# Queueing the late steps of an attention epilogue by estimated time

## The chip, the cores and the metric

The kernel runs on one NeuronCore of a Trainium2 chip, core 0. The metric is the device time of one launch in microseconds. A profiled execution gives the span and the records of every engine: TensorE (PE, with its weight loads as PEld), VectorE (DVE), ScalarE (ACT), GpSimd (POOL), and SyncE (SP), which issues the DMAs.

## The reference

Four transformer attention layers on a sequence of 2048 tokens with 512 features: 32 heads of 16 features. Layers 0 and 2 use the weights A and a sliding window of 256 keys; layers 1 and 3 use the weights B and attend to all 2048 keys, without a causal mask. Each layer adds its result to its input.

```python
def attn(x, wqkv, wo):                       # A: windowed, B: no mask
    qkv = (x @ wqkv).reshape(B, S, 3, H, Dh).transpose(2, 0, 3, 1, 4)
    q, k, v = qkv[0], qkv[1], qkv[2]
    scores = einsum("bhqd,bhkd->bhqk", q, k) * Dh ** -0.5
    mask = (idx[:, None] - idx[None, :] >= 0) & (idx[:, None] - idx[None, :] < 256)
    scores = where(mask[None, None], scores, -1e9)              # A only
    o = einsum("bhqk,bhkd->bhqd", softmax(scores), v)
    return o.transpose(0, 2, 1, 3).reshape(B, S, D) @ wo
x = A_x
for wqkv, wo in ((A_wqkv, A_wo), (B_wqkv, B_wo)) * 2:
    x = x + attn(layernorm(x), wqkv, wo)
```

## The kernel before

**Tiles.** The 2048 tokens are four chunks of 512 (`c` = 0 to 3), each of four token tiles of 128. The heads come in groups; one group of eight heads of one chunk, a quarter `t`, makes one `o` tile of 128 x 512. Names carry layer, chunk and part: `po2_3_1` is the output projection of layer 2, chunk 3, token tile 1. Numbers are split into a high and a low 16-bit half (`xh`, `oh`, `w`), so that a product takes three matmuls.

**One layer's work.** For a chunk: the layer norm (`st`, `mv`, the small operations of `rsqrt` in lines 44 to 51, then per tile `xn` and the two halves `xh`); `transpose` (PE `pt`, copies `xc`, high half by ACT, low half by DVE); `keys`, `queries`, `values` (PE `pq`, `pv`; halves `sp`, squares `sq`, norms of queries and keys `phq`, `phk`, from which DVE makes `km` and the shift `m`); attention (scores `s`, exponentials `e` by ACT, masks on POOL at L715 and L718 in the window layers, sums into one of two PSUM tiles `acc`); `epilogue`; and `wo` (PE `po`, then DVE `dx` = po x gcol at L567, and x + dx at L568). All of `pq`, `pv`, `po`, `pt` take a PSUM bank from the same small rotation, so a later one waits until DVE or ACT has read an earlier one.

**The epilogue.** It copies `acc` to `oe` (L599) and stores it; the denominators are read back as `lt`. Two later parts stand in a queue `late`. `reciprocals` makes the reciprocals on DVE and sends them through DRAM: `lt` to `rcp`, and `rcp` back, broadcast, as `r`. `normalised` multiplies `o` by `r` (L626) and splits the product into `oh` (L628, L629). In a window layer the first runs one step of the attention loop later, the second three; in a full layer three and five.

**The order.** PE's instruction order is written out by the program as it runs the loops; the other engines take their instructions in program order, moved by priorities in a few places. Beside the attention loop, `Side` holds a list of works for each chunk (`side0` for layer 0, and so on): transposes `T`, keys `K`, queries `Q`, values `VV`, output projections `OO`, norms `NN`, weight preparation `PR`. `Side.step` takes pieces of them between the steps of the attention, by their shares of cost. A work is taken when its dependencies are met by an estimated clock: `clock[0]`, which grows by an estimate for each piece; `ONR` holds the time from which `oh` counts as ready, and `XNR` the same for a norm. `Side.finish` takes what is left, and sets the clock forward when nothing is ready. The attention of a layer ends with `flush(0)` and `run_late(True)`, which forces all late parts; then `all_of` runs what must come before the next layer, the tail, for example values, the output projection of chunk 3, and the transposes and projections of the next layer's last chunk.

**Weights.** `maxima` finds column maxima (`wa` is a reduction over a weight's rows), `scales` makes powers of two, `parts` scales the weight (`wr`, on POOL), casts it to its high half (`w`, on DVE) and subtracts for the low half (POOL); one `yield` for each of four blocks. With `act` set the engines are DVE, ACT and POOL.

Of the kernel before, what the change touches and what calls it, by code (L numbers as in the profile page):

```python
# [38 lines left out]
def rsqrt(nc, vp, tag, var):  # L39

    v = vp.tile([P, 4], F32, name=f"v{tag}", tag="lnv")
    y = vp.tile([P, 4], F32, name=f"y{tag}", tag="lny")
    z = vp.tile([P, 4], F32, name=f"z{tag}", tag="lnz")
    nc.vector.tensor_scalar_add(v, var, EPS)
    nc.vector.tensor_scalar(y.bitcast(I32), v.bitcast(I32), 1, None, op0=ALU.logical_shift_right)
    nc.vector.tensor_scalar(y.bitcast(I32), y.bitcast(I32), -1, 0x5F3759DF, op0=ALU.mult, op1=ALU.add)
    for _ in range(3):
        nc.vector.tensor_mul(z, y, y)
# [141 lines left out]
def fast_path(ctx, tc, flag, a_x, a_wqkv, a_wo, b_wqkv, b_wo, out):  # L190
# [18 lines left out]
    CM, DN, WT, pend = {}, {}, {}, []  # L209

    clock, DONE, XNR, ONR = [0.0], {}, {}, {}
# [108 lines left out]
    def parts(ty, s, raw, act):  # L320

        dnb = DN.pop((ty, s))
        w = wp.tile([P, NC, 2, D], F16, name=f"w{ty}_{s}", tag="vf", bufs=NQ)
        for k in range(NC):
            r = raw[:, k, :]
            (nc.vector if act else nc.gpsimd).tensor_tensor(r, r, dnb, ALU.mult)  # L326
            if act:
                nc.scalar.activation(w[:, k, 0, :], r, AF.Copy)
            else:
                nc.vector.tensor_copy(w[:, k, 0, :], r)  # L330
# [62 lines left out]
    def norm(l, c, xs):  # L393

        st = vp.tile([P, 4, 6], F32, name=f"st{l}_{c}", tag="st")
        mv = vp.tile([P, 4, 2], F32, name=f"mv{l}_{c}", tag="mv")
        for i in range(4):
            nc.vector.bn_stats(st[:, i, :], xs[i])
            nc.vector.bn_aggr(mv[:, i, :], st[:, i, :])
        y = rsqrt(nc, vp, f"{l}_{c}", mv[:, :, 1])  # L400
        out = []
        for i in range(4):
            xn = vp.tile([P, D], F32, name=f"xn{l}_{c}_{i}", tag="xn", bufs=1)
            xh = vp.tile([P, 2, D], F16, name=f"xh{l}_{c}_{i}", tag="xh", bufs=XNB)
            norm1 = lambda o: nc.vector.tensor_scalar(o, xs[i], mv[:, i, 0:1], y[:, i:i + 1], op0=ALU.subtract, op1=ALU.mult)
            norm1(xn)
            norm1(xh[:, 0])
            nc.vector.tensor_tensor(xh[:, 1], xn, xh[:, 0], ALU.subtract)
            out.append(xh)
        XNR[l, c] = clock[0] + (0 if (l, c) == (0, 1) else 10)  # L410
        return out
# [10 lines left out]
    def transpose(l, c, xns, act):  # L422
        xc = XC[l, c] = wp.tile([P, 2, NC, QC], F16, name=f"xc{l}_{c}", tag="xc", bufs=NQ)
        for i in range(4):
            yield "wait", XNR[l, c] + 2.3 * i
# [9 lines left out]
            nc.vector.tensor_copy(lo, pt[:, 1])  # L435
            yield -spent(0.6)

# [119 lines left out]
    def wo(l, c):  # L557

        w = weights(l % 2, 3, f"o{l}_{c}")
        xs = load_x(l, c)  # L560
        yield wait(8)
        for i in range(4):
            ps = bank(f"po{l}_{c}_{i}")
            yield from mms(ps, [(O[l, c, t][:, a, i * P:(i + 1) * P], w[:, t, b, :]) for t in range(NHT) for a, b in TERMS])
            d = vp.tile([P, D], F32, name=f"dx{l}_{c}_{i}", tag="xn", bufs=1)
            k = 4 * c + i
            nc.vector.tensor_tensor(d, ps, gcol[l % 2], ALU.mult)  # L567
# [23 lines left out]
    def epilogue(l, c, qd, a, act):  # L591
# [17 lines left out]
        def reciprocals():  # L609
# [184 lines left out]
    class Side:  # L794
# [74 lines left out]
    def attention(l, works):  # L869
# [31 lines left out]
        run_late(True)  # L901
        PH["full"] = False

    def T(l, c, act=True):
        return Work(later(lambda: transpose(l, c, XN.pop((l, c)), act)), PT, ("T", l, c), [("N", l, c)])
# [29 lines left out]
    def NN(c, after=()):  # L935
        def gen():
            xs = load_x(0, c)
            yield wait(12 if c > 1 else 0)
            XN[0, c] = norm(0, c, xs)
# [6 lines left out]
    def all_of(works, following=()):  # L946
        Side(1, works, following).finish()

# [4 lines left out]
    XN[0, 0] = norm(0, 0, xs)  # L953
# [4 lines left out]
    run(transpose(0, 0, XN.pop((0, 0)), True))  # L958
# [27 lines left out]
    def side0(c):  # L986
# [6 lines left out]
        return [F(*[(qs[1, k], False) for k in range(NQ)]), OO(0, 2), VV(1, 0), VV(1, 1), T(1, 2), K(1, 2), Q(1, 0)]  # L993
# [77 lines left out]
```

## Time and profile before

| | |
|---|---|
| median of three runs | 2976.12 us (2972.74 to 2982.12) |
| profiled execution | 2971.72 us |
| its span | 2970.0 us |
| mean granted clock of PE | 0.979 |
| layer 0: window, tail | 93.1 to 545.0, 545.0 to 615.5 |
| layer 1: full attention | 615.5 to 1606.0 |
| layer 2: window, tail | 1606.0 to 1931.4, 1931.4 to 1987.2 |
| layer 3: full attention | 1987.2 to 2970.0 |

The first 93.1 us are the prologue: the first chunk's norm, the first weights, and the first projections. In the rows below, L12 is line 12 of the kernel before; `out<-in` are the program's names; a row of the timeline has start, duration, engine, line, operation, operands, count, and in brackets the engine's idle time before it with what ended it.

### The profile page before, as it was taken

The page shows a single profiled execution, that of the slowest core. Times are in us where ns is not written, and L with a number is a line of the kernel's source. Part 1 is how long each engine was busy: PE and PEld are TensorE (multiplying, and loading weights), DVE is VectorE, ACT ScalarE, POOL GpSimd, SP SyncE. Part 2 cuts the span into 40 slices and gives each one's busy share as a digit, 9 for nine tenths or more (in the row PEclk, how much of TensorE's full clock was granted, in tenths as well). Part 3 has the DMA queues.
Part 4 walks back from the last instruction along what each step waited for, and adds up shares of the span by engine and source line. Part 5 has one row for each costly group of instructions (what it writes and reads, how often), then busy time and mean ns, then how long its engine had stood idle before and what let it go on. Part 6 is the DMA issues. An engine that isn't in the chain of part 4 may idle for free.

```text
span 2970.0 us, 52024 instructions
## 1 busy us (share of the span) xinstructions
PE 2740.4 (92%) x20314; PEld 745.7 (25%) x20314; DVE 904.0 (30%) x1914; ACT 2400.6 (81%) x2703; POOL 561.7 (19%) x1127
## 2 busy tenths in 40 slices
PE   6778889899999999999999888899999999999996
PEld 3233333321122212212212333332112211121111
DVE  7656444401113112111212455631222222222112
ACT  3454555389999999999998666639999999999996
POOL 2456564100000000000002566600000000000000
PEclk8898999999999999999999999999999999999998
DMA  6575775532223233222222756542343334333331
GB/s 212 188 227 189 237 228 172 186 107 100 77 92 104 76 115 102 92 86 93 93 102 94 228 187 184 166 135 86 127 130 123 114 126 134 123 120 122 122 114 66
DMA packets 291409, 399.35 MB, mean 134 GB/s; under 512 B 70352, under 2 KB 173264, under 8 KB 283856
## 3 DMA queue, kind: packets, MB, share of 16 engines
q1 hardware_dynamic: 291152, 395.92, 41.0%
q8 instruction: 161, 2.64, 0.4%
q14 instruction: 96, 0.79, 0.1%
HBM read 263.19 MB, written 131.60 MB: 133 GB/s over the span
## 4 chain that ended last, share of the span: by engine, by line
PE 65%; ACT 10%; DMA 10%; DVE 7%; issue 4%; POOL 2%; SPq 1%; ACTq 0%; DVEq 0%; POOLq 0%
PE acc L693 26%; PE s L649 18%; ACT e L653 9%; PE acc L385 9%; PE pq L385 4%; DMA r<-rcp 4%; PE pv L385 3%; DMA rcp<-lt 2%; PE acc L725 2%; PE po L385 2%; DMA scr<-oe 1%; POOL wr L326 1%; DMA x<-in_A_x_dram 1%; POOL w L331 1%; DVE o L626 1%
## 5 line engine op out<-in xcount | busy, mean ns | idle before, releaser
L653 ACT ACTIVATE e<-s 128x1024 f32<-128x1024 f32 (+2 forms) x2432 | 2244.0, 1113 | 173.5 <-PE s L649 156.7
L693 PE MATMUL acc<-e,vt 128*17 128x512 f32 x8192 | 1078.5, 598 | 2.8 <-DVE oe L599 2.7
L649 PE MATMUL s<-qt,kt 64*128 64x512 f16 (+3 forms) x5504 | 797.1, 356 | 88.1 <-ACT e L653 16.6
L649 PEld LDWEIGHTS <-kt 64*128 64x128 f16 x5504 | 219.1, 94 | 953.0 <-issue 928.5
L718 POOL TENSOR_SCALAR_AFFINE_SELECT e<-e 128x256 f32<-128x256 f32 x512 | 229.0, 454 | 186.4 <-ACT e L653 185.5
L599 DVE COPY oe<-acc 128x512 f32<-128x512 f32 x128 | 88.0, 687 | 510.4 <-PE acc L693 449.2
L629 POOL TENSOR_TENSOR oh<-o,oh 128x512 f16<-128x512 f32 x32 | 37.1, 1159 | 1076.6 <-DVE oh L628 1060.9
L693 PEld LDWEIGHTS acc<-e,vt 128*17 128x17 f32 x8192 | 136.4, 95 | 349.0 <-issue 322.9
L715 POOL TENSOR_SCALAR_AFFINE_SELECT e<-e 128x256 f32<-128x256 f32 x448 | 195.4, 442 | 151.1 <-ACT e L653 148.1
L385 PE MATMUL pq<-xc,w 128*128 128x512 f16 x816 | 198.3, 397 | 20.0 <-DVE dx L567 5.3
L725 PE MATMUL acc<-e,vt 128*17 128x384 f32 (+2 forms) x2816 | 203.7, 396 | 5.4 <-POOL e L715 5.3
L385 PEld LDWEIGHTS <-w 128*128 128x128 f16 x1152 | 106.5, 100 | 254.5 <-issue 161.7
L626 DVE TENSOR_TENSOR o<-o,r 128x512 f32<-128x512 f32 x64 | 51.9, 811 | 352.4 <-DMA r<-rcp 344.7
L385 PE MATMUL po<-wo,oh 128*128 128x512 f16 x444 | 113.5, 409 | 39.1 <-DVE oh L628 19.2
L461 ACT ACTIVATE sp<-pq,es 128x512 f16<-128x512 f32 x68 | 46.6, 686 | 125.5 <-PE pq L385 106.2
L469 POOL TENSOR_TENSOR sq<-sp 128x512 bf16<-128x512 f16 x28 | 29.1, 1039 | 555.8 <-DVE sp L463 555.8
L385 PE MATMUL pv<-wv,xc 128*128 128x512 f16 x576 | 129.3, 379 | 0.5 <-ACT e L653 0.5
L552 ACT ACTIVATE vt<-pv 128x512 f32<-128x512 f32 x52 | 31.1, 597 | 118.5 <-PE pv L385 118.5
L385 PEld LDWEIGHTS <-oh 128*128 128x128 f16 x768 | 68.4, 101 | 207.5 <-issue 125.0
L385 PEld LDWEIGHTS <-xc 128*128 128x128 f16 x768 | 69.8, 98 | 135.2 <-issue 62.6
L463 DVE TENSOR_SCALAR sp<-acc,es 128x512 f16<-128x512 f32 x28 | 21.0, 751 | 267.6 <-PE acc L385 231.8
L385 PE MATMUL acc<-xc,w 128*128 128x512 f16 x336 | 93.8, 383 | 3.6 <-DVE sp L464 3.6
(129 smaller groups left out, 1478.3 us busy)
## 6 DMA issues: line engine op xcount, KB each, us to landing
kt<-kf SPq DMA_DIRECT2D x128, 512.0 KB
qt<-qs SPq DMA_DIRECT2D x128, 256.0 KB
scr<-oe SPq DMA_DIRECT2D x128, 256.0 KB
xd<-x SPq DMA_DIRECT2D x96, 256.0 KB
x<-xd SPq DMA_DIRECT2D x96, 256.0 KB
w<-wd SPq DMA_DIRECT2D x22, 1024.0 KB
kt<-kw SPq DMA_DIRECT2D x64, 256.0 KB
o<-scr SPq DMA_DIRECT2D x64, 256.0 KB
```

What stands on the lines that cost most here:

```text
L385: nc.tensor.matmul(ps, a, b, start=(i == 0), stop=(i == len(pairs) - 1))
L461: nc.scalar.activation(sp[:, 0], ps, AF.Copy, scale=e)
L552: nc.scalar.activation(vt[:, i, :, :DH], src, AF.Copy)
L599: nc.vector.tensor_copy(oe, a)
L626: nc.vector.tensor_tensor(o, o, r, ALU.mult)
L629: (nc.gpsimd if l % 2 else nc.vector).tensor_tensor(ohl[:, 1], o, ohl[:, 0], ALU.subtract)
L649: nc.tensor.matmul(ps[:, h, s0:s0 + wd_], kt[R * h:R * h + R, pr, kc:kc + P], qt[R * h:R * h + R, pr, qc:qc + wd_], start=True, stop=True)
L653: nc.scalar.activation(e[:, :, w0:w1], ps[:, :, w0:w1], AF.Exp, scale=SCALE)
L693: nc.tensor.matmul(a[32 * h:32 * h + DH + 1, :], V[l, j // 4][:, j % 4, 4 * qd + h, :], es_[h // 2][:, h % 2, :], start=(j == 0), stop=(j ...
L715: nc.gpsimd.affine_select(v, v, pattern=[[0, 2], [-1, P]], compare_op=ALU.is_gt, fill=0.0, base=0, channel_multiplier=1)
L718: nc.gpsimd.affine_select(v, v, pattern=[[0, 2], [1, P]], compare_op=ALU.is_ge, fill=0.0, base=0, channel_multiplier=-1)
L725: nc.tensor.matmul(a[32 * h:32 * h + DH + 1, q * P:(q + nb) * P], V[l, (4 * c + j) // 4][:, j % 4, 4 * qd + h, :], es_[h // 2][:, h % 2, s ...
```

## The change

Four things are changed together.

1. Late parts carry a due time of the estimated clock: `reciprocals` 4.5 us after the epilogue, `normalised` 8 us after the reciprocals. `run_late` takes all that are due, in each step of the attention and before each piece of `Side.one`. The attention's end no longer forces them; `all_of` ends with a `run_late(True)` that sets the clock forward. When nothing is ready in `Side.one`, the clock goes to the next late part's time if that comes first.
2. `parts` casts block k − 1 while it scales block k.
3. The norm is split: `stats` is called for each token tile as it is made (in `wo`, in `NN`, in the prologue), and `norm` for one tile at a time in `transpose`, two tiles ahead of the PE transposes, with ready times from `LN` (clock + 7, then 2 us per tile). `wo` loads `x` after the wait for its weight.
4. `rsqrt` takes three operations an iteration instead of four. In `side0(3)`, `VV(1, 0)` comes ahead of `OO(0, 2)`.

```diff
     for _ in range(3):
-        nc.vector.tensor_mul(z, y, y)
-        nc.vector.tensor_mul(z, z, v)
-        nc.vector.tensor_scalar(z, z, -0.5, 1.5, op0=ALU.mult, op1=ALU.add)
-        nc.vector.tensor_mul(y, y, z)
+        nc.vector.tensor_mul(z, y, v)
+        nc.vector.scalar_tensor_tensor(z, z, -0.5, y, op0=ALU.mult, op1=ALU.mult)
+        nc.vector.scalar_tensor_tensor(y, z, 1.5, y, op0=ALU.add, op1=ALU.mult)
...
-        for k in range(NC):
-            r = raw[:, k, :]
-            (nc.vector if act else nc.gpsimd).tensor_tensor(r, r, dnb, ALU.mult)
-            if act:
-                nc.scalar.activation(w[:, k, 0, :], r, AF.Copy)
-            else:
-                nc.vector.tensor_copy(w[:, k, 0, :], r)
-            nc.gpsimd.tensor_tensor(w[:, k, 1, :], r, w[:, k, 0, :], ALU.subtract)
+        for k in range(NC + 1):
+            if k < NC:
+                r = raw[:, k, :]
+                (nc.vector if act else nc.gpsimd).tensor_tensor(r, r, dnb, ALU.mult)
+            if k:
+                r, (hi, lo) = raw[:, k - 1, :], (w[:, k - 1, b, :] for b in range(2))
+                if act:
+                    nc.scalar.activation(hi, r, AF.Copy)
+                else:
+                    nc.vector.tensor_copy(hi, r)
+                nc.gpsimd.tensor_tensor(lo, r, hi, ALU.subtract)
             yield
...
-    def norm(l, c, xs):
...
+    def stats(l, c, i, x):
+
+        if i == 0:
+            ST[l, c] = (vp.tile([P, 4, 6], F32, name=f"st{l}_{c}", tag="st"),
+                        vp.tile([P, 4, 2], F32, name=f"mv{l}_{c}", tag="mv"), [])
+        st, mv, xs = ST[l, c]
+        xs.append(x)
+        nc.vector.bn_stats(st[:, i, :], x)
+        nc.vector.bn_aggr(mv[:, i, :], st[:, i, :])
+        if i == 3:
+            del ST[l, c]
+            LN[l, c] = clock[0] + 7.0
+            XN[l, c] = (xs, mv, rsqrt(nc, vp, f"{l}_{c}", mv[:, :, 1]))
+
+    def norm(l, c, i):
+
+        xs, mv, y = XN[l, c]
...
+        norm1(xn)
+        norm1(xh[:, 0])
+        nc.vector.tensor_tensor(xh[:, 1], xn, xh[:, 0], ALU.subtract)
+        return xh
...
-    def transpose(l, c, xns, act):
+    def transpose(l, c, act):
+
+        xns, ready = [], []
+        def ahead():
+            xns.append(norm(l, c, len(xns)))
+            ready.append(max([clock[0] + 1.0, LN[l, c]] + ready[-1:]) + 2.0)
+        ahead()
+        ahead()
         xc = XC[l, c] = wp.tile([P, 2, NC, QC], F16, name=f"xc{l}_{c}", tag="xc", bufs=NQ)
         for i in range(4):
-            yield "wait", XNR[l, c] + 2.3 * i
+            if ready[i] > clock[0]:
+                yield "wait", ready[i]
...
+            if i < 2:
+                ahead()
             yield -spent(0.6)
+        del XN[l, c]
...
         w = weights(l % 2, 3, f"o{l}_{c}")
+        yield wait(8)
+
         xs = load_x(l, c)
-        yield wait(8)
...
-            nc.sync.dma_start(out[0, k * P:(k + 1) * P, :] if l == 3 else xd[k], xs[i])
+            nc.sync.dma_start(xd[k], xs[i])
+            stats(l + 1, c, i, xs[i])
             yield -MM if PH["full"] else -12 * MM
-        if l < 3:
-            XN[l + 1, c] = norm(l + 1, c, xs)
...
-            late.append([5 if l % 2 else 3, normalised])
-        late.append([3 if l % 2 else 1, reciprocals])
+            late.append((clock[0] + 8, normalised))
+        late.append((clock[0] + 4.5, reciprocals))
 
     def run_late(done=False):
 
-        while late and (done or late[0][0] <= 0):
-            late.popleft()[1]()
-        for x in late:
-            x[0] -= 1
+        for _ in range(len(late)):
+            x = late.popleft()
+            if done:
+                clock[0] = max(clock[0], x[0])
+            if x[0] <= clock[0]:
+                x[1]()
+            else:
+                late.append(x)
+        if done and late:
+            run_late(True)
...
+            run_late()
             at = [(w.ready_at(), i) for i, w in enumerate(self.q)]
             at = [(r, i) for r, i in at if r is not None]
+            if force and late and not any(r <= clock[0] for r, _ in at):
+                t = min(x[0] for x in late)
+                if not at or t <= min(at)[0]:
+                    clock[0] = max(clock[0], t)
+                    return 0.0
...
         flush(0)
-        run_late(True)
         PH["full"] = False
...
         Side(1, works, following).finish()
+        run_late(True)
...
-    XN[0, 0] = norm(0, 0, xs)
+    for i in range(4):
+        stats(0, 0, i, xs[i])
...
-        return [F(*[(qs[1, k], False) for k in range(NQ)]), OO(0, 2), VV(1, 0), VV(1, 1), T(1, 2), K(1, 2), Q(1, 0)]
+        return [F(*[(qs[1, k], False) for k in range(NQ)]), VV(1, 0), OO(0, 2), VV(1, 1), T(1, 2), K(1, 2), Q(1, 0)]
```

More of the change, by code (lines that the diff above doesn't have):

```diff
@@ L208, in fast_path @@
     XC, XN, V, O, KM, EP, PH = {}, {}, {}, {}, {}, {}, {"full": False}
-    CM, DN, WT, pend = {}, {}, {}, []
-    clock, DONE, XNR, ONR = [0.0], {}, {}, {}
+    CM, DN, WT, ST, LN, pend = {}, {}, {}, {}, {}, []
+    clock, DONE, ONR = [0.0], {}, {}
     def spent(us):
@@ L389, in fast_path @@
     TERMS = ((0, 0), (0, 1), (1, 0))
-    def norm(l, c, xs):
[L395 to L411, printed above, removed]
+    def stats(l, c, i, x):
[12 more added lines that the diff above has]
+        xs, mv, y = XN[l, c]
+        xn = vp.tile([P, D], F32, name=f"xn{l}_{c}_{i}", tag="xn", bufs=1)
+        xh = vp.tile([P, 2, D], F16, name=f"xh{l}_{c}_{i}", tag="xh", bufs=XNB)
+        norm1 = lambda o: nc.vector.tensor_scalar(o, xs[i], mv[:, i, 0:1], y[:, i:i + 1], op0=ALU.subtract, op1=ALU.mult)
+        norm1(xn)
+        norm1(xh[:, 0])
+        nc.vector.tensor_tensor(xh[:, 1], xn, xh[:, 0], ALU.subtract)
+        return xh
     def load_x(l, c):
@@ L938, in gen @@
             yield wait(12 if c > 1 else 0)
-            XN[0, c] = norm(0, c, xs)
+            for i in range(4):
+                stats(0, c, i, xs[i])
             yield 0.0
@@ L952, in fast_path @@
     fill(qs[0, 0], False)
-    XN[0, 0] = norm(0, 0, xs)
+    for i in range(4):
+        stats(0, 0, i, xs[i])
     run(maxima(0, 1, raw[1], False))
@@ L957, in fast_path @@
     run(maxima(0, 0, raw[0], False))
-    run(transpose(0, 0, XN.pop((0, 0)), True))
+    run(transpose(0, 0, True))
     sc = scales(0, 0)
```

2 lines of the change are left out of this document (1 added, 1 removed).

## The prediction

> **What bounds the kernel now.** I read the page first (engine totals, chain of work that ended last), then the busy time by stage, then the waits, and last the timeline of the few places where the changed order differs. First the page: the span, the engines' busy time, and the chain's shares.
>
> ```profile
> span 2970.0 us, 52024 instructions
> PE 2740.4 (92%) x20314; PEld 745.7 (25%) x20314; DVE 904.0 (30%) x1914; ACT 2400.6 (81%) x2703; POOL 561.7 (19%) x1127
> PE 65%; ACT 10%; DMA 10%; DVE 7%; issue 4%; POOL 2%; SPq 1%; ACTq 0%; DVEq 0%; POOLq 0%
> ```
>
> PE is busy 92% of the span, but that is an average over seven stages. The table by stage gives, after the stretch and its length, busy time of PE, PEld, DVE, ACT and POOL, then the granted clock, the DMA share and GB/s. The stages are prologue, windowed attention of layer 0, the tail before layer 1, full attention of layer 1, and the same three for layers 2 and 3.
>
> ```profile
> 0.00:93.10 93.10, 53.94 (x238) 26.92 (x239) 64.83 (x136) 25.70 (x40) 18.99 (x27) 0.88 0.63 209
> 93.10:545.00 451.90, 383.93 (x3234) 160.81 (x3236) 240.87 (x499) 247.59 (x321) 253.21 (x527) 0.95 0.65 206
> 545.00:615.50 70.50, 61.51 (x294) 27.05 (x291) 30.50 (x70) 17.69 (x28) 0.32 (x1) 0.93 0.56 190
> 615.50:1606.00 990.50, 967.82 (x6892) 203.87 (x6891) 168.52 (x383) 948.63 (x1025) 47.46 (x46) 1.00 0.27 92
> 1606.00:1931.40 325.40, 276.29 (x2723) 112.57 (x2720) 168.94 (x384) 202.31 (x246) 195.11 (x483) 0.96 0.60 187
> 1931.40:1987.20 55.80, 50.74 (x255) 22.80 (x255) 26.76 (x64) 11.48 (x19) 0.00 (x0) 1.00 0.50 160
> 1987.20:2970.00 982.80, 946.21 (x6690) 191.73 (x6689) 203.54 (x379) 947.20 (x1025) 46.60 (x43) 0.99 0.35 115
> ```
>
> In the two full-attention stages PE and ACT are both nearly full. The changed program has PE's instructions in the same order there, and DVE's the same around every wait but for two copies taken earlier, so 1973 of the 2970 us get 0. What can move lies elsewhere: PE is idle 39.2 us in the prologue, 68.0 in window 0 (451.90 − 383.93), 49.1 in window 2, and 9.0 and 5.1 in the tails.
>
> The waits of the whole run (waiting instruction, releaser, total, times, longest) show what the change aims at:
>
> ```profile
> DVE o L626 <- DMA r<-rcp: 344.7, 57, 10.6
> PE po L385 <- DVE dx L567: 18.6, 7, 5.3
> DVE w L330 <- POOL wr L326: 22.0, 8, 5.3
> ```
>
> DVE stands 344.7 us in front of the normalising multiply, because it is queued before the reciprocals have come back by DMA. Most of that costs nothing. It costs where something PE needs is queued behind the multiply: `dx`, which frees a PSUM bank for the output projection (18.6 us), an `xc` copy, or a `km` reduction.
>
> **Prologue.** The change splits the norm into `stats` and `norm`, and takes the reduction `m` ahead of the reduction `wa` of a weight that comes late.
>
> ```profile
> 82.50 0.40 PE L486 MATMUL phq_None<-sq,hsum 128*32 128x512 bf16 x4
> 93.11 0.82 PE L649 MATMUL s<-qt,kt 64*128 64x384 f16 x4 [10.21 <-DMA qt<-qs]
> ...
> 83.47 3.62 DVE L285 TENSOR_REDUCE wa<-wr 128x512 f32<-128x2048 f32 x1 [3.68 <-DMA wr<-in_B_wqkv_dram]
> 87.00 0.74 DVE L517 TENSOR_SCALAR m_None<-phq_None,kx 128x512 f16<-128x512 f32 x1
> ```
>
> `phq` is finished at 82.9; `m` runs at 87.00 only because the 3.62 us reduction, itself waiting for a load, is in front. In the new order `m` runs at about 83.0. Its DMA to `qs`, the load of `qt` and the first score matmul follow it on one chain, so they gain 4.0. The weight's column reductions no longer stand behind the norm's subtractions and the rsqrt has three operations fewer; I estimate 1.4 from that. Against this, the new PE order takes the first scores and `acc` ahead of the transposes of the next chunk, which filled waiting time: 2 given back. Sum −3.4; bounds −6 and 0.
>
> **Windows 0 and 2.** Here `reciprocals` and `normalised` wait for 4.5 and another 8 us of estimated time instead of one and three steps. An example of what goes, chunk 3 of layer 2:
>
> ```profile
> 1916.48 1.04 PE L649 MATMUL s<-qt,kt 64*128 64x384 f16 x8 [6.10 <-DVE xc L435]
> ...
> 1885.23 0.94 DVE L626 TENSOR_TENSOR o<-o,r 128x512 f32<-128x512 f32 x1 [1.18 <-DMA r<-rcp]
> 1912.81 0.69 DVE L626 TENSOR_TENSOR o<-o,r 128x512 f32<-128x512 f32 x1 [4.21 <-DMA r<-rcp]
> ```
>
> The multiply at 1912.81 waits 4.21 us; behind it are a subtraction and the `xc` copy for which PE idles 6.10. In the new order that multiply comes later and the 6.10 go. But the multiply at 1885.23 then stands before `dx2_2_1` instead of behind it, and `po2_2_2` needs that `dx` to free its bank. `r` still lands near 1885.2, so `po2_2_2` starts some 2 us later than now. The transposes of chunk 2 are two turns earlier and meet a norm that isn't finished; following DVE's new queue, I estimate waits of 3.0, 1.5 and 1.6 at two transposes and the projection. So −6.1 + 2 + 6.1: about +2. The other places of window 2, worked in the same way, give −1.7 (`po` no longer behind `oh` of layer 1), −1 and −0.5 at two transposes, and one stall at a `km` that turns into one at a squared projection. Sum −1; bounds −6 and +4.
>
> In window 0 most of the bursts of `dx` waits keep a multiply in front of some `dx`; I get −1.5 at one multiply, −0.5 at a second. The weight casts add cost: now DVE waits 22.0 us for POOL's scaling before each cast. A turn later DVE no longer waits, but POOL is given all scalings and subtractions of a weight ahead of a mask that PE needs, and a `sp` subtraction stands behind four casts; the longest single such wait was 5.3, I put the price at half, +2.5. With a weight maximum behind another multiply (+0.5) the sum is +1; bounds −6 and +8, because this is many small shifts.
>
> **The tails.** This is where the order itself speaks against the change. Before, the attention ends with all late parts forced, so `po` of chunk 3 was ready at once, and the values and a projection ran behind it. Tail 2 on PE, then the norm on DVE:
>
> ```profile
> 1931.37 10.53 PE L385 MATMUL pv<-wv,xc 128*128 128x512 f16 x48
> 1944.36 8.02 PE L385 MATMUL po<-wo,oh 128*128 128x512 f16 x35 [0.51 <-DVE oh L628]
> 1953.08 10.52 PE L385 MATMUL pv<-wv,xc 128*128 128x512 f16 x48
> 1963.44 2.75 PE L385 MATMUL pq_h<-xc,w_h 128*128 128x512 f16 x12
> 1966.44 0.62 PE L429 MATMUL pt<-ident,xh 128*128 128x128 f16 x8
> 1969.15 1.05 PE L429 MATMUL pt<-ident,xh 128*128 128x128 f16 x16 [1.26 <-ACT sq_h L467]
> 1970.93 2.99 PE L385 MATMUL pq_h<-xc,w_h 128*128 128x512 f16 x12 [0.73 <-ACT xc L432]
> ...
> 1953.28 0.69 DVE L567 TENSOR_TENSOR dx<-po,gcol 128x512 f32<-128x512 f32 x1 [0.23 <-PE po L385]
> 1955.68 0.17 DVE L44 TENSOR_SCALAR v<-mv 128x4 f32<-128x4 f32 x1
> 1956.29 0.16 DVE L48 TENSOR_TENSOR z<-y 128x4 f32<-128x4 f32 x1
> 1958.67 0.55 DVE L405 TENSOR_SCALAR xn<-x,mv,y 128x512 f32<-128x512 f32 x1
> 1960.05 0.69 DVE L408 TENSOR_TENSOR xh<-xn,xh 128x512 f16<-128x512 f32 x1
> 1968.87 0.74 DVE L435 COPY xc<-pt 128x512 f16<-128x512 f16 x2
> ```
>
> From the end of the last `po` (1953.05) to the first finished `xh` (1960.74) DVE needs 7.7 us, and the 10.52 of `pv` plus 3.0 of projection and `phk` cover it: the transposes wait only 1.26 and 0.73. In the new order the fillers come first, since the estimate does not yet hold `oh` to be ready, then `po`, and directly behind it the transposes. PE would reach `pt` with nothing to do. In numbers from 1931.4: pv, pv, projection and po take 1966.44 − 1931.37 − 0.51 = 34.6. Then 0.2 + 2.4 to the start of rsqrt (1953.28 to 1955.68), 12 operations at 0.20 (from 1955.68 to 1958.67 are 15), and 2.1 to the first `xh` (1958.67 to 1960.74): 7.1. Three more tiles, at about 1.7 each with their copies between, let the last `pt` start at 12.5, and the projection 1.4 after it, at 13.9. So it starts 48.5 us into the tail, where it started 39.5: +9.0.
>
> Tail 0, in which a `po` wait of 3.35 goes:
>
> ```profile
> 561.16 10.57 PE L385 MATMUL po<-wo,oh 128*128 128x512 f16 x39 [3.35 <-DVE oh L628]
> 571.57 2.75 PE L385 MATMUL pq<-xc,w 128*128 128x512 f16 x12
> 582.56 0.61 PE L429 MATMUL pt<-ident,xh 128*128 128x128 f16 x8
> 589.13 4.50 PE L385 MATMUL pq<-xc,w 128*128 128x512 f16 x12 [0.68 <-ACT xc L432]
> ```
>
> From 557.8, where the wait begins: the projections take 582.52 − 571.57 = 10.95, `po` 10.4, and the same 13.9 end at 593.1, where it is 589.13 now: +4.0.
>
> Idle PE also costs clock. The twelve matmuls at 589.13 took 4.50 behind gaps of a few us, the twelve at 1970.93 took 2.99 behind 0.73; the tails' clocks are 0.93 and 1.00. With 7 us idle in tail 2 I add 4.50 − 2.99 = +1.5. [...]
>
> **The sum.** Prologue −3.4, window 0 +1, window 2 −1, tails +9.0 + 4.0 + 1.5 = +14.5, full attention 0: +11. Against the profiled execution, 2971.7 us (the span and 1.7 around it), that is 2983; that run lies 4.4 below the median of three, 2976.1, so against the median it is 2987. A change below 0.3%, 9 us, can hardly be told from none.
>
> **The rivals.** *The windows win.* If the moved multiplies leave no new wait, the gain is the whole of 18.6 (`dx`) and 6.1 (`xc`) and the prologue's 3.4: −28, with the tails −13.6, so 2962 (with bounds of 8 either way, 2954 to 2970). It decides when over about 23 of these 28 are real. For it: the stalls are on PE, each with its row. Against it: in the new order a multiply still stands before `dx2_2_1` and others. Chance 0.17.
>
> *They cancel.* The same mechanism at half, −14, or tails that cost less, because the norm's operations fall between others: 2976, within 0.3%. That also holds if the timed queue merely puts the multiplies elsewhere and the tails' fillers end up behind `po`. Chance 0.33, with the low end of my own sum.
>
> *Masks held back by casts.* If the 22.0 us that DVE waited come back as POOL queues ahead of masks, and half of it reaches PE, +11 on top: 2998. It is an end of the range and part of the 0.50 for slower.
>
> **How the numbers follow.** My forecast, 2987, has its own range from the bounds: prologue ±3, windows ±8 together, tails ±2.5, taken as independent ±9, so 2978 to 2996. The range for all takes in the upper part of the first rival and ends just past the last: 2966 to 3000. Faster 0.17; same 0.33, since the band up to 2985 holds the second rival and the low third of my forecast; slower 0.50.
>
> **What would show it.** Right: in tail 2 PE idles some 7 us in front of the first `pt`, and again between the four, released by DVE, and the tail is 65 us long; tail 0 is 74 to 76; the first score at about 89.7; no 6.10 wait of a score for `xc` in chunk 3, but one of `po` for `dx`; full attention within 2 us. Wrong: if window 0 or 2 is shorter by over 8 us, `po` no longer waits for `dx`, and the multiplies' 344.7 us fall to a small part with nothing late in their place; or if the tails show `pv` between `po` and `pt`.

## The result, and the profile after

The changed kernel takes 2992.86 us in the median of 8 runs (2985.04 to 3001.39), the kernel before 2977.22 in the median of 8 beside it. The ratio is 1.0053, with a 95% interval of 1.0035 to 1.0071, so about +16 us. In the rounds of a later experiment it was 1.0067 (1.0046 to 1.0087). The forecast was 2987, with a range of 2966 to 3000. The profiled execution shown here took 2998.08; its span is 2996.4.

First the page of the changed kernel: span, busy time of the engines, shares of the chain that ended last.

```profile
span 2996.4 us, 51979 instructions
PE 2757.5 (92%) x20314; PEld 751.0 (25%) x20314; DVE 895.1 (30%) x1866; ACT 2402.0 (80%) x2703; POOL 557.5 (19%) x1127
PE 65%; ACT 10%; DVE 9%; DMA 9%; issue 4%; POOL 2%; SPq 1%; ACTq 0%; DVEq 0%; POOLq 0%
```

DVE has the 48 operations of rsqrt less, and 9 us less work; its share of the chain has risen from 7 to 9%. Then busy time by stage, the columns as before: prologue, window 0, tail 0, layer 1, window 2, tail 2, layer 3.

```profile
0.00:85.00 85.00, 55.12 (x238) 27.55 (x239) 61.98 (x128) 25.92 (x40) 19.34 (x27) 0.90 0.67 225
85.00:542.60 457.60, 389.66 (x3238) 162.20 (x3239) 240.23 (x486) 247.27 (x321) 248.50 (x527) 0.94 0.64 205
542.60:614.10 71.50, 60.58 (x286) 26.93 (x284) 30.47 (x67) 17.56 (x27) 0.32 (x1) 0.90 0.54 182
614.10:1609.40 995.30, 969.23 (x6895) 203.63 (x6896) 167.32 (x373) 949.86 (x1025) 47.42 (x46) 1.00 0.27 91
1609.40:1941.90 332.50, 279.21 (x2725) 113.61 (x2723) 164.45 (x370) 202.51 (x246) 195.25 (x483) 0.93 0.59 183
1941.90:2013.70 71.80, 58.36 (x254) 25.38 (x252) 27.02 (x63) 11.71 (x19) 0.00 (x0) 0.83 0.39 123
2013.70:2996.40 982.70, 945.36 (x6690) 191.74 (x6689) 203.59 (x379) 947.19 (x1025) 46.63 (x43) 0.99 0.35 115
```

Tail 2 has grown from 55.8 to 71.8 us and its granted clock has fallen from 1.00 to 0.83; window 2 from 325.4 to 332.5. The prologue is 8 us shorter. To see which differences are more than one execution's, I took the stages from a second profile of each kernel too, each stage running from the start of one named matmul to another (the tail from its first projection, so 0.3 to 1 us off the rows above):

| stage | before | before, second | changed | changed, second | second − second |
|---|---|---|---|---|---|
| prologue | 93.1 | 92.8 | 85.0 | 84.0 | −8.8 |
| window 0 | 452.3 | 454.6 | 457.6 | 457.7 | +3.1 |
| tail 0 | 69.6 | 69.8 | 71.6 | 71.5 | +1.7 |
| layer 1 | 990.9 | 991.3 | 995.2 | 992.4 | +1.1 |
| window 2 | 325.5 | 324.7 | 332.5 | 330.8 | +6.1 |
| tail 2 | 55.8 | 55.7 | 71.8 | 69.9 | +14.2 |
| layer 3 | 974.0 | 974.4 | 973.1 | 974.4 | 0.0 |

The second pair adds up to +17.4, between the 15.6 of the medians above and the 20.4 of its own rounds. The extra of the first pair lies in layer 1, window 2 and tail 2 of the changed kernel and in window 0 of the kernel before. In the rounds of `e1_tail` to `e4_rsqrt` below the kernel before had a median of 2986.58, in those of the second pair, `e7_steps_tail` and `e8_cast` 2972.67, so across them times are compared by ratios, and a difference of a few us in a stage is weak evidence.

The waits of the whole run answer to the three shown of before:

```profile
DVE o L644 <- DMA r<-rcp: 368.0, 61, 11.3
PE po L387 <- DVE dx L586: 29.3, 6, 7.8
DVE w L332 <- POOL wr L326: 14.1, 7, 3.6
```

This is the most important reading. Queueing by time was to take the multiply away from the DMA that it waits for; it waits no less than before, 368.0 against 344.7 us, and PE waits for `dx` 29.3 instead of 18.6. In the second pair it is 350.0 against 342.1, and 26.1 against 19.1. Of each of the four sums for the multiply, 234 to 240 us belong to the full-attention layers; DVE's idle time before the 32 multiplies of the window layers is 117.4 before and 121.7 changed (second pair).

Tail 2 on PE, from the last sums of the attention:

```profile
1941.92 20.89 PE L387 MATMUL pv<-wv,xc 128*128 128x512 f16 x96
1962.65 2.75 PE L387 MATMUL pq_h<-xc,w_h 128*128 128x512 f16 x12
1967.78 12.22 PE L387 MATMUL po<-wo,oh 128*128 128x512 f16 x48 [2.38 <-DMA wo<-wd]
1985.88 0.61 PE L444 MATMUL pt<-ident,xh 128*128 128x128 f16 x4 [5.88 <-DVE xh L414]
1988.91 1.03 PE L444 MATMUL pt<-ident,xh 128*128 128x128 f16 x8 [0.94 <-DVE xh L417]
1991.94 0.61 PE L444 MATMUL pt<-ident,xh 128*128 128x128 f16 x4 [0.48 <-DVE xh L417]
1993.24 5.31 PE L387 MATMUL pq_h<-xc,w_h 128*128 128x512 f16 x12 [0.69 <-ACT xc L447]
```

Two blocks of values and a projection run first, then `po`, and PE stands 5.88 us before the first transpose and again before the later ones. Two things here the prediction did not have: `po` waits 2.38 us for its own weight, and the projection behind the transposes takes 5.31 us, where it took 2.99 and 4.50 was expected. The next rows are stretches of the same tail:

```profile
1980.00:1993.20 13.20, 4.32 (x33) 3.10 (x33) 11.56 (x31) 2.39 (x4) 0.00 (x0) 0.58 0.61 190
1993.20:2003.00 9.80, 7.62 (x20) 2.32 (x20) 2.93 (x6) 1.37 (x2) 0.00 (x0) 0.67 0.25 70
2003.00:2013.70 10.70, 10.70 (x45) 4.41 (x43) 0.00 (x0) 1.79 (x3) 0.00 (x0) 0.86 0.61 200
```

The clock is 0.58 while DVE normalises (11.56 of 13.20 us busy), and 0.67 and 0.86 in the stretches after it. These are means. Cut where the granted clock changes, the same tail shows only half and full:

```profile
1968.40:1971.80 3.40, 3.40 (x9) 1.20 (x8) 0.00 (x0) 0.00 (x0) 0.00 (x0) 0.50 0.19 70
1982.10:1999.20 17.10, 10.16 (x45) 4.77 (x46) 10.07 (x31) 3.00 (x5) 0.00 (x0) 0.50 0.38 124
1999.20:2002.60 3.40, 1.37 (x6) 0.51 (x6) 2.14 (x5) 0.76 (x2) 0.00 (x0) 1.00 0.69 195
2002.60:2006.00 3.40, 3.40 (x9) 1.22 (x8) 0.28 (x1) 0.09 (x1) 0.00 (x0) 0.50 0.61 165
```

The first half-clock stretch lies behind `po`'s wait of 2.38, the second begins 2.1 us into the idle time that starts at 1980.0, and the last lies behind a wait of 2.15.

The third place is `po` in chunk 3 of window 2, on DVE, then on PE:

```profile
1886.55 0.18 DVE L403 BATCH_NORM_AGGREGATE mv<-st 128x2 f32<-128x6 f32 x1
1893.00 0.69 DVE L644 TENSOR_TENSOR o<-o,r 128x512 f32<-128x512 f32 x1 [6.27 <-DMA r<-rcp]
1893.61 0.68 DVE L586 TENSOR_TENSOR dx<-po,gcol 128x512 f32<-128x512 f32 x1
...
1894.35 3.15 PE L387 MATMUL po<-wo,oh 128*128 128x512 f16 x7 [7.85 <-DVE dx L586]
```

The multiply of `o2_3_1` now stands before `dx2_2_1`, waits 6.27 us for `r`, and PE stands 7.85 us before its next `po`. Measured from the first score of chunk 3, that `po` starts at 36.6 us where it started at 31.7 (35.9 and 31.5 in the second pair).

### The profile page after: what moved, and what is told of

Its sections match the earlier page's. It is cut to its first block, busy times and chain, and to the rows that moved or that the text cites. A ratio compares the mean times of both kernels' runs of the same rounds, so it can differ in the third digit from the quotient of the medians.

```text
span 2996.4 us, 51979 instructions
## 1 busy us (share of the span) xinstructions
PE 2757.5 (92%) x20314; PEld 751.0 (25%) x20314; DVE 895.1 (30%) x1866; ACT 2402.0 (80%) x2703; POOL 557.5 (19%) x1127
## 4 chain that ended last, share of the span: by engine, by line
PE 65%; ACT 10%; DVE 9%; DMA 9%; issue 4%; POOL 2%; SPq 1%; ACTq 0%; DVEq 0%; POOLq 0%
PE acc L717 25%; PE s L673 18%; PE acc L387 9%; ACT e L677 9%; PE pq L387 4%; PE pv L387 4%; DMA r<-rcp 4%; DMA rcp<-lt 3%; PE po L387 2%; PE acc L749 2%; DVE xh L417 1%; DMA scr<-oe 1%; DVE o L644 1%; DVE xh L414 1%; DVE xn L414 1%
## 5 line engine op out<-in xcount | busy, mean ns | idle before, releaser
L673 PE MATMUL s<-qt,kt 64*128 64x512 f16 (+3 forms) x5504 | 798.7, 357 | 83.7 <-ACT e L677 14.2
L742 POOL TENSOR_SCALAR_AFFINE_SELECT e<-e 128x256 f32<-128x256 f32 x512 | 223.7, 444 | 209.1 <-ACT e L677 208.4
L739 POOL TENSOR_SCALAR_AFFINE_SELECT e<-e 128x256 f32<-128x256 f32 x448 | 194.3, 439 | 143.1 <-ACT e L677 140.6
L644 DVE TENSOR_TENSOR o<-o,r 128x512 f32<-128x512 f32 x64 | 53.2, 832 | 368.2 <-DMA r<-rcp 368.0
L387 PE MATMUL po<-wo,oh 128*128 128x512 f16 x444 | 113.9, 413 | 46.0 <-DVE dx L586 29.3
L479 ACT ACTIVATE sp<-pq,es 128x512 f16<-128x512 f32 x68 | 46.7, 687 | 108.6 <-PE pq L387 82.6
L387 PEld LDWEIGHTS <-oh 128*128 128x128 f16 x768 | 69.2, 101 | 213.3 <-issue 138.8
L570 ACT ACTIVATE vt<-pv 128x512 f32<-128x512 f32 x52 | 31.1, 597 | 110.1 <-PE pv L387 110.1
L387 PEld LDWEIGHTS <-xc 128*128 128x128 f16 x768 | 70.5, 99 | 140.7 <-issue 70.0
```

Source lines behind the costliest of these rows:

```text
L387: nc.tensor.matmul(ps, a, b, start=(i == 0), stop=(i == len(pairs) - 1))
L479: nc.scalar.activation(sp[:, 0], ps, AF.Copy, scale=e)
L644: nc.vector.tensor_tensor(o, o, r, ALU.mult)
L673: nc.tensor.matmul(ps[:, h, s0:s0 + wd_], kt[R * h:R * h + R, pr, kc:kc + P], qt[R * h:R * h + R, pr, qc:qc + wd_], start=True, stop=True)
L739: nc.gpsimd.affine_select(v, v, pattern=[[0, 2], [-1, P]], compare_op=ALU.is_gt, fill=0.0, base=0, channel_multiplier=1)
L742: nc.gpsimd.affine_select(v, v, pattern=[[0, 2], [1, P]], compare_op=ALU.is_ge, fill=0.0, base=0, channel_multiplier=-1)
```

## The experiments

**The tails' order, `e1_tail`.** The values and the query projection of each tail get the same dependency as the output projection; nothing else of the changed kernel is touched.

```diff
-    tails = {0: [OO(0, 3), VV(1, 2), Q(1, 1), T(1, 3), K(1, 3)],
-             2: [OO(2, 3), VV(3, 1), VV(3, 2), Q3(0, 0, True), T(3, 3), K3(3, 0, True)]}
+    tails = {0: [OO(0, 3), VV(1, 2), Q(1, 1, True, [("O", 0, 3, NHT - 1)]), T(1, 3), K(1, 3)],
+             2: [OO(2, 3), VV(3, 1), VV(3, 2, True, [("O", 2, 3, NHT - 1)]),
+                 Q3(0, 0, True, [("O", 2, 3, NHT - 1)]), T(3, 3), K3(3, 0, True)]}
```

> The changed kernel with one edit: in both tails the values and the query projection that had slipped ahead of the output projection po wait for the same time as po, so that po comes after the first values again and the fillers stand between po and the transposes. Theory A (the tails' order is the main loss): tail 2, from the end of window 2 to the first score of layer 3, falls from 71.8 us to 55 to 58, the 5.88 gap ahead of the first pt and the 2.38 wait of po for its weight go; tail 0 falls by 2 to 4; the whole comes to 2975 to 2980, against 2993. Theory B (the loss is the windows' and the clock's): tails shorten, but the whole stays above 2986.

Ratio 0.9997 (0.9985 to 1.0008), where the change as it is has 1.0053 to 1.0067. That is theory A's size; tail 2 is 58.7, just above its 55 to 58, and tail 0 67.8. PE in tail 2:

```profile
1961.36 8.88 PE L387 MATMUL po<-wo,oh 128*128 128x512 f16 x39 [1.28 <-DVE oh L646]
1970.08 10.52 PE L387 MATMUL pv<-wv,xc 128*128 128x512 f16 x48
1983.03 1.06 PE L444 MATMUL pt<-ident,xh 128*128 128x128 f16 x16
1987.29 4.30 PE L387 MATMUL pq_h<-xc,w_h 128*128 128x512 f16 x12 [0.69 <-ACT xc L447]
```

The values stand between `po` and `pt` again, the gap is gone, and so is the wait for the weight, whose load now is issued ahead. The tails' order accounts for the size of the whole loss. What remains of the change comes out even, but not because it does nothing: in this profile the prologue is 7.6 us shorter and the windows are longer, 460.9 and 337.5.

**One part of the change at a time, on the kernel before.** Each edit is that part of the change's diff; cut to what marks it:

```diff
-            late.append([5 if l % 2 else 3, normalised])     # e2_time, with run_late,
+            late.append((clock[0] + 8, normalised))          # Side.one and the end unforced
...
-            XN[l + 1, c] = norm(l + 1, c, xs)                # e3_norm, with norm by
+            stats(l + 1, c, i, xs[i])                        # token tile in transpose
...
-        nc.vector.tensor_scalar(z, z, -0.5, 1.5, op0=ALU.mult, op1=ALU.add)             # e4_rsqrt,
+        nc.vector.scalar_tensor_tensor(z, z, -0.5, y, op0=ALU.mult, op1=ALU.mult)       # three for four
...
-        for k in range(NC):                                  # e8_cast: block k - 1 is cast
+        for k in range(NC + 1):                              # while block k is scaled
```

> The kernel before with only the due times: late parts by estimated clock, no forced end of the attention. Norm, casts and rsqrt as before. Theory A (due times make both the tails' order and the dx wait): tail 2 +12 to +17, tail 0 +2 to +4, window 2 +3 to +7 with po2_2_2 waiting 6 to 8 us for dx2_2_1; prologue 0; the whole 2993 to 3000. Theory B (the split norm is what the tails wait for): tail 2 at most +5, the whole below 2985.

> The kernel before with only the split norm (stats for each tile in wo, norm in the transposes two tiles ahead, x loaded behind the weight wait); late parts by steps and forced, casts and rsqrt as before. Theory A: prologue -6 to -8 (m ahead of the late weight's reduction), tail 2 +4 to +8, as po comes behind two blocks of values and only a projection covers the norm, windows within 3; the whole 2972 to 2980. Theory B (the split norm causes window 2's loss, transposes waiting for xh): window 2 +6 or more, the whole above 2985.

> The kernel before with only the three-operation rsqrt. Theory A: it saves 0.6 us for each norm on VectorE, and m comes ahead of the late weight's reduction in the prologue, -6 to -8 there; no stage longer; the whole 2966 to 2971. Theory B (the fused operations on 128x4 take longer, or the prologue's gain is given back in window 0, as in the changed kernel): within 3 us of before.

> The kernel before with only the weight casts a turn later. By the prediction's step: VectorE's 22.0 us of waits for GpSimd's scaling fall to a few, and the burst of the first weight in window 0 costs +2.5, ratio 1.0005 to 1.0015. Rival (the cast is beside the path): VectorE's wait falls, every stage within 1 us, ratio 0.9995 to 1.0005.

| stage | before, second | e2_time | e3_norm | e4_rsqrt | e8_cast |
|---|---|---|---|---|---|
| prologue | 92.8 | 92.3 | 86.4 | 86.4 | 93.6 |
| window 0 | 454.6 | 461.3 | 458.9 | 459.2 | 455.3 |
| tail 0 | 69.8 | 73.7 | 68.9 | 69.2 | 66.6 |
| layer 1 | 991.3 | 992.9 | 999.3 | 994.2 | 990.2 |
| window 2 | 324.7 | 331.9 | 333.9 | 331.0 | 322.9 |
| tail 2 | 55.7 | 70.5 | 65.9 | 57.4 | 55.5 |
| ratio | | 1.0079 | 1.0031 | 0.9992 | 1.0005 |
| 95% interval | | 1.0061 to 1.0097 | 1.0018 to 1.0044 | 0.9974 to 1.0009 | 0.9991 to 1.0019 |

The column "before, second" is from other rounds than `e2_time` to `e4_rsqrt`.

`e2_time`: theory A; the due times alone make both tails' loss (+14.8 and +3.9) and PE's wait for `dx2_2_1` (7.9). Window 0, of which nothing was expected, is 6.7 longer. The stretch from `s2_3_3` to `s2_3_4` is 27.8 instead of 17.9, but it is not the same work: it holds 48 matmuls of `po` here and in the changed kernel, and 36 in the kernel before. `e3_norm`: both theories in part. The prologue gains 6.4 as expected, but tail 2 loses more than expected, 10.2: `po` slips behind the second block of values here too, so only a projection covers the norm. Either of the two parts is thus enough to spoil tail 2.

```profile
1968.17 10.52 PE L385 MATMUL po<-wo,oh 128*128 128x512 f16 x48
1978.53 2.75 PE L385 MATMUL pq_h<-xc,w_h 128*128 128x512 f16 x12
1985.71 0.61 PE L442 MATMUL pt<-ident,xh 128*128 128x128 f16 x4 [4.43 <-DVE xh L412]
```

And window 2 loses 9, theory B's size but not its reason: it is the first chunk that is long (86.8 against 74.6), where no transpose waits for `xh`. There, on DVE, the multiply `o2_0_5` has come before the last `sp` of a projection, as in the changed kernel:

```profile
1697.01 0.69 DVE L642 TENSOR_TENSOR o<-o,r 128x512 f32<-128x512 f32 x1 [5.39 <-DMA r<-rcp]
...
1698.81 0.74 DVE L480 SCALAR_TENSOR_TENSOR sp<-pq,es,sp 128x512 f16<-128x512 f32 x1
```

That this slip makes the 12 us is not shown: PE's clock in the chunk is 0.94 instead of 1.00, too. Why its layer 1 is 8 us longer stays open.

`e4_rsqrt`: 6.4 of prologue, and at the end 2.4 us by the ratio, theory B; the interval still allows theory A's smallest gain. The program's order of DVE's work did not change, but its order on the engine did, also among operations that the edit does not touch. First the prologue, where `m` is now ahead of the reduction, then chunk 1 of window 2 (DVE, then PE):

```profile
79.75 0.75 DVE L516 TENSOR_SCALAR m_None<-phq_None,kx 128x512 f16<-128x512 f32 x1 [2.85 <-PE phq_None L485]
80.42 3.61 DVE L284 TENSOR_REDUCE wa<-wr 128x512 f32<-128x2048 f32 x1
...
1775.04 0.69 DVE L625 TENSOR_TENSOR o<-o,r 128x512 f32<-128x512 f32 x1 [5.67 <-DMA r<-rcp]
...
1776.12 4.72 PE L384 MATMUL pq_h<-xc,w_h 128*128 128x512 f16 x11 [4.19 <-DVE xc L434]
```

The multiply `o2_1_5` has slipped between two `xc` copies, and the projection waits 4.19 for the second. So what stands above on the engines' order (the program's order, moved by priorities) holds for PE alone: DVE's order is made by the framework's scheduler, and a small edit can deal out new places to the multiplies. That the scheduler goes by its own estimate of when operands are ready is the likeliest reading, but no run shows it.

`e8_cast`: nearer the rival, though 1.0005 is where both ranges meet and the interval holds both; no effect of the cast can be told from none. DVE's wait for POOL's scaling fell only from 22.1 to 14.5, not to a few, and the stages did not stay within 1 us: tail 0 is 3.2 shorter, the first chunk of window 0 6.7 us shorter and the second 6.2 longer.

The due times, the split norm and the short rsqrt each lengthen window 2 by 6 to 9 us alone, each with its own pattern of chunks, and the whole change does so by 6.1. The parts do not add up. `VV(1, 0)` ahead of `OO(0, 2)` was not run by itself.

**The same kernels again**, `e5_before` and `e6_after`, are the second profiles of the result.

> The kernel before, unchanged, for a second profile on the chip that the variants run on. Theory A (the stages without a changed order differ from run to run by a few us): layer 1, which took 990.9 in the first profile and 994 to 999 in the variants, takes 994 or more here too, and window 2 is longer by 3 to 6 than in the first profile. Theory B (the variants themselves lengthen layer 1 and window 2): layer 1 is 991 again, window 2 325.

> The changed kernel, unchanged, timed in the same rounds as the variants. Its ratio to before should be again 1.004 to 1.007; tail 2 is 70 to 72, tail 0 71 to 72, the stretch from s2_3_3 to s2_3_4 28 against 18 before.

Theory A fails: layer 1 and window 2 of the kernel before repeat within 1 us. But theory B is not shown for layer 1 either, since `e7_steps_tail` and `e8_cast`, in the same rounds as this profile, have 992.5 and 990.2. The changed kernel has the ratio and tail 0 expected; tail 2 with 69.9 and the stretch with 26.6 are a little below.

**The due times taken out**, `e7_steps_tail`: the tails' order of `e1_tail`, and `late` by steps with a forced end as before.

```diff
-            late.append((clock[0] + 8, normalised))
-        late.append((clock[0] + 4.5, reciprocals))
+            late.append([5 if l % 2 else 3, normalised])
+        late.append([3 if l % 2 else 1, reciprocals])
...
         flush(0)
+        run_late(True)
```

> The changed kernel with late parts by steps and a forced end, as before, and the tails' order restored as in e1_tail: split norm, cast a turn later and short rsqrt remain. Theory A (due times cost 10 us in window 2, where the multiply of o2_3_1 stands before dx2_2_1): against e1_tail the stretch from s2_3_3 to s2_3_4 falls from 26 to 18, the whole is 4 to 8 below e1_tail, ratio to before 0.997 to 0.9985. Theory B (stalls only move: what the due times cost there they save elsewhere): ratio 0.9990 to 1.0010.

Ratio 0.9988 (0.9977 to 0.9999); the stretch from `s2_3_3` is 17.6, with 36 matmuls of `po` again. The place is theory A's; the size is between the two theories, and the interval holds both. Window 2 as a whole stays long, 334.7, because its first chunk is 86.4 against 82.6 in `e1_tail`. So the due times explain the stall at `dx2_2_1`, but not by themselves the 6.1 us of window 2.

**Does the due time place the multiply?** `e9_due14` is `e1_tail` with 14 for 8 in the window layers. `e10_pin8` and `e11_pin14` tie the multiply on DVE behind all that the program wrote before it, with 8 and with 14.

```diff
-            late.append((clock[0] + 8, normalised))
+            late.append((clock[0] + 14 if l % 2 == 0 else clock[0] + 8, normalised))   # e9, e11
...
-                nc.vector.tensor_tensor(o, o, r, ALU.mult)
+                m = nc.vector.tensor_tensor(o, o, r, ALU.mult)                            # e10, e11
+                if l % 2 == 0:
+                    tc.keep_in_program_order(m)
```

> e1_tail with the multiply due 14 us after the reciprocals in the window layers instead of 8. Theory A (the due time places the multiply only in the order in which the program is written; VectorE's own order is set by the framework's scheduler, which expects the reciprocals back too early): VectorE's waits for r in the two window layers, 122 to 128 us over 28 to 30 of the 32 multiplies in the changed kernel, stay above 95, and the ratio to before is 0.998 to 1.001, as e1_tail. Theory B (8 us is simply too short): the waits fall below 60, ratio 0.994 to 0.997.

> e1_tail with each multiply of the window layers pinned in VectorE's queue behind all that the program wrote before it, due time 8 as in the change. Theory A (the place on VectorE is what counts): the waits for r fall to 60 to 100, the stretch from s2_3_3 to s2_3_4 from 26 to 16 to 19, as the multiply of o2_3_1 then stands behind dx2_2_2; ratio 0.996 to 0.999. Rival (stalls only move): waits as before within 15, ratio 0.9990 to 1.0010.

> As e10_pin8 with a due time of 14. Theory A: the waits for r fall below 50, windows 0 and 2 together 8 to 20 us shorter than in e1_tail, ratio 0.993 to 0.997. Rival (the normalised halves come late, and the output projection, the norm and the transposes behind them with them): waits gone, but windows within 4 us of e1_tail, ratio 0.999 to 1.002.

| | changed, second | e1_tail | e9_due14 | e10_pin8 | e11_pin14 |
|---|---|---|---|---|---|
| DVE idle before the 32 multiplies | 121.7 | 137.4 | 122.6 | 50.2 | 15.2 |
| window 0 | 457.7 | 460.9 | 448.4 | 449.4 | 427.3 |
| window 2 | 330.8 | 337.5 | 327.4 | 307.3 | 309.1 |
| ratio | 1.0067 | 0.9997 | 0.9938 | 0.9883 | 0.9808 |
| 95% interval | 1.0046 to 1.0087 | 0.9985 to 1.0008 | 0.9920 to 0.9955 | 0.9863 to 0.9903 | 0.9788 to 0.9827 |

With 14 instead of 8 the waits stay long, 122.6 where `e1_tail` has 137.4 and the changed kernel 121.7: on that theory A was right. That the time would stay was wrong: the due time also sets from when `oh` counts as ready, so PE's order changes, and its waits for `dx` nearly go (the changed kernel's second profile, then `e9_due14`; `e1_tail` has 27.5):

```profile
PE po L387 <- DVE dx L586: 26.1, 6, 6.4
```

```profile
PE po L387 <- DVE dx L586: 3.8, 3, 2.5
```

Pinned, the due time acts. `e10_pin8` has less wait and more gain than expected, and `e11_pin14` more gain. PE's matmuls start in the same order in `e1_tail` and `e10_pin8`, and in `e9_due14` and `e11_pin14`, but for 24 and 32 records of 20314, so what the pin gains does not come from PE's order. Waits of DVE for `r` in window 2 of `e9_due14`, then of `e11_pin14`:

```profile
DVE o L644 <- DMA r<-rcp: 63.9, 14, 9.4
```

```profile
DVE o L644 <- DMA r<-rcp: 5.7, 1, 5.7
```

What is left there is the last multiply of layer 1, which is not pinned and runs in the first 15 us of window 2. Of the 32, only the last one of each window layer still waits, 8.3 and 6.9 us, in the tails. The stages of `e11_pin14`, windows and tail 2:

```profile
84.80:512.20 427.40, 380.96 (x3239) 160.33 (x3240) 238.21 (x483) 247.33 (x321) 251.09 (x527) 0.95 0.69 221
1567.30:1876.40 309.10, 275.78 (x2724) 112.25 (x2722) 165.08 (x369) 202.15 (x246) 199.28 (x483) 0.96 0.63 195
1876.40:1935.60 59.20, 54.40 (x253) 23.77 (x251) 27.76 (x64) 11.49 (x19) 0.00 (x0) 0.94 0.49 159
```

PE is idle 46.4 us in window 0 where it was idle 68.0 before the change, and 33.3 in window 2 where it was 49.1. At 2920 us this version is 57 us below the kernel before in its own rounds and, by the ratios, some 2.4% below the changed one.

**What of that is the multiplies' place, without the other parts?** `e12_before_pin14`: the kernel before with due times, 14, the pin and a forced end: `e2_time` with the 14 and the pin of `e11_pin14`, and with `run_late(True)` kept behind `flush(0)` in place of the tails' dependencies.

> The kernel before with due times (14 for the multiply in the window layers), the pinned multiply and a forced end of the attention; norm in one piece, casts and rsqrt as before. Theory A (e11_pin14's gain is the multiplies' place and little else): waits for r in the window layers below 30, windows 20 to 30 us shorter, prologue 0, ratio 0.983 to 0.988. Rival (the gain needs the split norm, whose operations otherwise stand in a row before the dx and xc that PE waits for): ratio 0.990 or more, with waits of PE for the norm in the windows.

Ratio 0.9861 (0.9837 to 0.9884), theory A: 18.1 us before the 32 multiplies, windows 431.8 and 305.0, prologue 92.5. The other parts of the change, the tails mended, are worth the 0.5% between 0.9861 and 0.9808, whose intervals just do not touch; half of that is the prologue's 7.7 us. The pin without any due time was not run, so how the gain divides between the two is open.

## Why the prediction was right, and where it was wrong

The sign and the main step were right: the tails' order speaks against the change and decides. That the sum came within 6 us, +11 against +17.4, is partly luck: the prologue's miss of −5.4 and the windows' of +9.2 work against each other. The second pair of profiles gives each term. Three views of rows that the list needs: the first matmuls of `po` in tail 0 of the kernel before, PE in tail 0 of the changed kernel, and a multiply of window 2 of each kernel.

```profile
555.71 2.10 PE L385 MATMUL po<-wo,oh 128*128 128x512 f16 x9
...
563.77 10.52 PE L387 MATMUL po<-wo,oh 128*128 128x512 f16 x48
580.17 0.61 PE L444 MATMUL pt<-ident,xh 128*128 128x128 f16 x4 [5.88 <-DVE xh L414]
587.52 5.31 PE L387 MATMUL pq<-xc,w 128*128 128x512 f16 x12 [0.69 <-ACT xc L447]
...
1867.83 5.52 DVE L626 TENSOR_TENSOR o<-o,r 128x512 f32<-128x512 f32 x1 [4.43 <-DMA r<-rcp]
1872.76 7.05 DVE L644 TENSOR_TENSOR o<-o,r 128x512 f32<-128x512 f32 x1 [3.71 <-DMA r<-rcp]
```

- **Tails, +14.5 forecast, +15.9.** The sum hides two misses, +14.2 for +10.5 in tail 2 and +1.7 for +4.0 in tail 0. In tail 2 the projection started 13.2 after `po`'s end (forecast 13.9), at 1993.24 in the first profile, where `po` ended at 1980.0. Mis-sized were two terms. The tail up to `po`'s end took 38.1 instead of 34.6; 2.4 of that is `po`'s wait for its weight, whose load takes the buffer that the second block of values frees, and which issues at 1962.85, just behind that block, and 1.7 is `po` itself, 12.22 instead of 10.5, with the half clock behind that wait (10.53 in the second profile). The step that failed is the move of `po`: I had moved its PE work, not the load that goes with it. And the clock cost more than 1.5: the projection alone 5.31 − 2.99 = 2.3, and the tail from its start to layer 3 grew from 16.2 to 20.5. The clock went to half at 1982.1, in the 5.88 us gap, and it was at half behind idle of only 2.38 and 2.15 us, too; from the gap on it stayed there for 17.1 us, with short waits between the transposes, where the prediction's 1.5 counted one slowed projection. Tail 0 came to +1.7, not +4: the wait of 3.35 went, as forecast, and the projection started 13.2 behind `po`'s end there, too. But the forecast counted 2.1 us twice: it began at 557.8, behind the first nine matmuls of `po`, and still gave `po` its whole 10.4. The projection lost 0.8 us, 5.31 for 4.50.
- **Prologue, −3.4 forecast, −8.8.** `m` did come ahead, and the first score at 85.0 instead of 93.1. In the first profiles PE's wait before that score fell by 4.75, for the 4.0 of `m`; 1.4 for the shorter norm was too little, as the first projection starts 3.3 earlier, at 31.1; and the 2 us counted as given back do not show in the prologue. Nor do they show in the first chunk of window 0, which is 3.6 us shorter.
- **Window 0, +1 forecast, +3.1.** Within its bounds, but not for its reason: the cast, put at +2.5, measured nothing by itself, and DVE's wait for POOL's scaling did not go (14.1 of 22.1). By chunks the window changed by −3.6, +5.6, −0.8 and +1.9; `e8_cast` by itself has −6.7 and +6.2 in the first two, so the cast moves time there rather than adding any.
- **Window 2, −1 forecast, +6.1.** Outside its bounds. The `po` wait for `dx2_2_1` came as forecast, 7.85, but the price was "some 2 us" and that `po` came 4.9 later in its chunk (4.4 in the second pair); `e2_time`, with 4.6, shows that this is the due times' work. I had set the multiply's release at a fixed time, 1885.2, but it ran at 1893.0. Of these 7.8 us, 4.7 are the chunk's own later start. Another 1.5 are the reciprocals, which ran in both kernels as soon as `lt` had come, but later in the chunk, because one multiply in front of them, `o2_2_7`, took still longer than before, 7.05 for 5.52 us. The other multiplies of window 2 take 0.69 to 0.94; through this one POOL's masks run without a break, and no run tests whether they are the reason. The last 1.5 are the way of `r` itself, 8.5 instead of 7.0. By chunks window 2 changed by +5.5, −6.5, +2.4 and +4.7, so its sum is no single stall.
- **Full attention, 0, and +1.1 and 0.** Right.
- **The rivals.** "The windows win" was turned down for the right reason, a multiply still before `dx`; the pinned kernels show that its 28 us were too few for the case in which the multiplies do leave: in `e12_before_pin14` the two windows are 42.5 shorter. "They cancel" names the case in which the fillers end up behind `po`; the change did not take it, and `e1_tail`, which does, has 0.9997. "Masks held back by casts" did not happen: PE's waits for POOL's masks fell from 5.3 to 1.1.

Of the signs named, PE's idle time before the transposes and the exchange of the 6.10 for a wait for `dx` held; the lengths of the tails (71.8 for 65, 71.6 for 74 to 76), the first score (85.0 for 89.7) and, in the first profile, layer 1 (+4.3 for 2) did not.

One reading ran through the prediction without being tested in it: that the change takes the multiplies out of their waits. By DVE's waits it does not.

## What to carry to other kernels

When an edit delays work by a planner's clock, look first whether that clock sets the engine's order: the row to watch is the engine's wait for that DMA, which here did not fall below that of the kernel before until the instruction was pinned. A wait of an engine that is 30% busy is worth attention when anything that the bottleneck needs is queued behind it. And when work is reordered around a latency, count what stands between producer and consumer after the move, on every queue: here the blocks on the wrong side of `po` cost the tails 15.9 us, nearly the whole loss.

## What the runs showed of the hardware

In a stretch of tail 2 of the changed kernel in which PE had 4.32 us of work in 13.20 the mean granted clock was 0.58, then 0.67 and 0.86 over the next 20 us, and the same twelve matmuls took 5.31 us instead of the 2.99 of the kernel before. In this tail the clock took only the values 0.50 and 1.00. It was at half for 17.1 us, and it also went to half behind single waits of 2.38 and 2.15 us. The round trip from the reciprocals on DVE through DRAM to the start of the multiply took 8.0 us in layer 2 and 9.0 in layer 0, in the median of the multiplies that waited for `r` in the changed kernel's second profile. In the runs with at least seven such multiplies in a layer the medians are 7.6 to 8.3 in layer 2 and 8.6 to 10.0 in layer 0.
